# Attention, Fourier mixing and feed-forward block on one core: key memories and scores first in batch 0, half tiles in column halves, weights' sums and splits pulled ahead

## The chip, the cores and the metric

One Trainium2 chip, one core. The metric is the device time of one execution in microseconds (us); three runs of the kernel before were timed. An instruction of the trace belongs to TensorE (PE; its weight loads are PEld), VectorE (DVE), ScalarE (ACT), GpSimd (POOL) or to SyncE's DMA queue (SP).

## The reference

```python
a = exp(phi - max(phi, axis=2)); a = a / (sum(a, axis=2) + 1e-9)   # phi: B 8, H 8, S 576, M 32
k_m = einsum('bhsm,bhsd->bhmd', a, k)                              # memories, 32 per head
v_m = einsum('bhsm,bhsd->bhmd', a, v)
attn = softmax(q @ k_m.T / 8) @ v_m                                # B, H, S, D 64
x = attn.transpose(0, 2, 1, 3).reshape(B, S, 512)
u = x + real(fft(fft(x, axis=1), axis=2))
un = (u - mean(u)) / sqrt(var(u) + 1e-6)                           # over the 512
out = u + relu(un @ w_ch1) @ w_ch2                                 # 512 -> 2048 -> 512
```

## The kernel before, in words

Per batch (8 of them, 4 pairs of heads each) `background` makes attention and mixing: `pooling_weights` (the exponentials of phi, transposed), `pair_memory` (tiles pm: keys' and values' memories), `pair_scores` (tiles psc, softmax, and the even and odd sums `aeo` that the transform over tokens needs, L485 to L522), `values` (values times the transform over the model, pv, then vh), `spectrum` (pa, then at), and for each token tile `mix_m` (the mixing product pp, cosine part in columns 0 to 256 and sine part in the other 255) and `mix_x` (px, the attention output itself), added by `add_mix` (L654). A batch has 576 tokens, so four full tiles of 128 and one half tile of 64 rows; two batches share a tile with their halves.

Two token tiles form a chunk (18 chunks). Each is normed (`norm_tile`, `norm_chunk`), and goes through the feed-forward part in 8 weight blocks of 256 inner columns. Products are made from high and low f16 parts, three per product (`ffn1`, `ffn2`); batches 0 and 1 and the first chunk take f32 products instead, which the trace shows as two records each (`ffn1_direct` L712: 8 products a block, `ffn2_direct` L729: 4 a block).

The weights arrive as 64-bit words and become f32 on the chip in `to_f32`: ACT's L808, DVE's L810 and L811 (sign), and for the low word either DVE's L821, or, for the keys in the list `LP` (four blocks of the second weight), DVE's L816 and an addition on POOL (L819). Each block's squares are then summed (ACT L830, a matmul with ones in `all_sum`, tile as_sq), which gives the scale (`norm_scale`, L232 to L243); `split_w1`, `scale_w2` and `prepare_w2` make the f16 parts. The first chunk runs beside this conversion, block by block.

A scheduler places the instructions of each engine by modelled times. Its order is bent by `tc.high_priority(n)`, which pulls what is issued within it ahead, and by `tc.issue_after(x)`, which holds an instruction until x has been issued. `GATE1` and `GATE2` name for each weight block such marks: "un1" and "uh0" belong to the first chunk's norm, "s0_3" is set by the last score operation of batch 0 (L522). The small constants mk come by a DMA of SP, as do phi, the pairs, the transform tables (vt, ct) and the weights.

Of the kernel before, what the change touches and what calls it, by code (L numbers as in the profile page):

```python
# [20 lines left out]
P = 128  # L21
# [21 lines left out]
KEEP = [8, 18, 0, 0, 22, 4, 3]  # L43
GATE1 = [[]] + [["un1", "uh0"]] * 7
GATE2 = [["un1", "uh0"]] * 8
NA = 2
# [7 lines left out]
L2 = [2, 4, 6]  # L54
LP = ["2_0", "2_2", "2_4", "2_6"]
W1_STAGE = ["w4", "w6", "s1", "w6", "s1", "s2", "s1", "x"]
# [76 lines left out]
def kernel(  # L133
# [200 lines left out]
    def pooling_weights(b):  # L334
# [28 lines left out]
        for g in range(2):  # L363
# [7 lines left out]
            )  # L371

    def pair_memory(b, g, r, vmf, ivs):

# [3 lines left out]
        if b < NX:  # L378
            pm = psg.tile([P, 512], F32, tag="g", name=f"pm_{n}")
            mm = groups()  # L380
            for w in range(2):
                for t in range(NST):
                    mm(
                        pm[:, w * 64 : w * 64 + 64],
                        lhsT=kv[:, t, w, :],
                        rhs=et32[:, g // 2, t, 64 * (g % 2) : 64 * (g % 2) + 64],
                        start=(t == 0),
                        stop=(t == NST - 1),
                    )
            kmf = share[:, g * 64 : g * 64 + 64] if b == 0 else tiny("kmf", 64, 2)  # L390
            nc.vector.tensor_tensor(out=kmf, in0=pm[:, 0:64], in1=mk[:, 0:64], op=ALU.mult)
            nc.vector.tensor_tensor(
                out=vmf[:, g],
                in0=pm[:, 64:128].unsqueeze(1).to_broadcast([P, 2, 64]),
                in1=mk[:, 0:64].unsqueeze(1).to_broadcast([P, 2, 64]),
                op=ALU.mult,
            )
            return q, None, kmf, 1.0 / 8.0
        am = tiny("am", 3, 1)
# [218 lines left out]
    def mix_m(b, key, cols, rows, at, vh, beta, qscale):  # L618

        pp = psg.tile([P, 512], F32, tag="g", name=f"pp_{b}_{key}")  # L620
        mm = groups()
        for cs in range(2):
            js = slice(0, NJ) if cs == 0 else slice(NJ, DM)
            i = 0
            for kb in range(2):
                for la, lv in ((0, 0), (1, 0), (0, 1)):
                    mm(
                        pp[rows, js],
                        lhsT=at[:, (kb * 2 + cs) * 2 + la, cols],
                        rhs=vh[:, lv, kb, js],  # L630
                        start=(i == 0),
                        stop=(i == 5),
                    )
                    i += 1
        qs = qsb[qi[0] % 2]
        qi[0] += 1
        nc.scalar.activation(qs[rows, 1 : NJ - 1], pp[rows, NJ:DM], AF.Copy, scale=qscale[rows])  # L637
# [163 lines left out]
    def to_f32(stages, dst, key):  # L801
# [27 lines left out]
        sq = tiny("sq", 2, 4)  # L829
        marks["sq" + key] = nc.scalar.activation(elt.rearrange("p l c -> p (l c)").bitcast(BF16)[:, :UW], dst, AF.Square, accum_out=sq[:, 0:1])  # L830
        return all_sum(sq[:, 0:1], 1, f"sq_{key}")

# [16 lines left out]
    def prepare_w1(j):  # L849

        t = w1_f32(j)
        top = to_f32(parts_w1.pop(j), t, f"1_{j}")
        s = s1[:, j : j + 1]
        norm_scale(s, is1[:, j : j + 1], top, 1, 9, f"w1_{j}")

# [3 lines left out]
    def stage_w2(j):  # L859
        top = to_f32(parts_w2.pop(j), w2_f32(j), f"2_{j}")  # L860
        norm_scale(s2[:, j : j + 1], is2[:, j : j + 1], top, 1, 14, f"w2_{j}")

# [29 lines left out]
    def background():  # L892
# [3 lines left out]
        for b in range(B):  # L896
# [6 lines left out]
            yield (nt if half_made is None else half_made), 0  # L903
            if b == 0:
                for g in range(NG):
                    mem[g] = pair_memory(b, g, first[g], vmf, ivs)
            for step in range(NG + 2):
                if step < NG and b > 0:
                    r = load_pair(b, step)
                if step >= 2 and b > 0:  # L910
# [4 lines left out]
                if step < NG and b > 0:  # L915
                    mem[step] = pair_memory(b, step, r, vmf, ivs)
                    yield (nt if half_made is None else half_made), 0
# [33 lines left out]

    nc.sync.dma_start(out=mk, in_=mk_d)
    load_phi(0)
# [20 lines left out]
    def after(names, fn, *a):  # L974
        with ExitStack() as st:
            for m in names:
                st.enter_context(tc.issue_after(marks[m].ins))
            return fn(*a)

    gate = ["un1", "uh0"]  # L980

# [13 lines left out]
    for j in range(NW):  # L995
# [105 lines left out]
```

## Time and profile before

| | us |
|---|---|
| median of 3 runs (lowest, highest) | 981.11 (980.9, 982.27) |
| the profiled execution's own time | 980.04 |
| its span in the profile | 978.2 |

| engine | busy us | share of the span |
|---|---|---|
| PE | 937.8 | 96% |
| DVE | 570.7 | 58% |
| ACT | 456.0 | 47% |
| POOL | 229.9 | 23% |

The shares are means over stages that differ. The mean granted clock of TensorE is 0.989 of full speed. A row of the timeline is one instruction or a run of equal ones, with its start in us from the span's start, what it wrote and read, and in brackets the idle time of its engine before it and what ended that.

### The profile page before, as it was taken

The page shows a single profiled execution, that of the slowest core. Times are in us where ns is not written, and L with a number is a line of the kernel's source. Part 1 is how long each engine was busy: PE and PEld are TensorE (multiplying, and loading weights), DVE is VectorE, ACT ScalarE, POOL GpSimd, SP SyncE. Part 2 cuts the span into 40 slices and gives each one's busy share as a digit, 9 for nine tenths or more (in the row PEclk, how much of TensorE's full clock was granted, in tenths as well). Part 3 has the DMA queues.
Part 4 walks back from the last instruction along what each step waited for, and adds up shares of the span by engine and source line. Part 5 has one row for each costly group of instructions (what it writes and reads, how often), then busy time and mean ns, then how long its engine had stood idle before and what let it go on. Part 6 is the DMA issues. An engine that isn't in the chain of part 4 may idle for free.

```text
span 978.2 us, 18885 instructions
## 1 busy us (share of the span) xinstructions
PE 937.8 (96%) x7753; PEld 664.3 (68%) x7753; DVE 570.7 (58%) x1301; ACT 456.0 (47%) x910; POOL 229.9 (23%) x249
## 2 busy tenths in 40 slices
PE   9388898989999999999999999999999999999998
PEld 6256577666687667676767776767677667666664
DVE  3889958757655765776623666657655765311111
ACT  2455448695555544755431645565545543401110
POOL 1213324334221422333120223123311321300000
PEclk9699999999999999999999999999999999999999
DMA  9706564064225430465111632164214310210000
GB/s 351 282 7 265 180 173 131 1 140 122 62 50 99 116 88 29 88 127 122 39 23 36 122 107 68 44 120 122 69 44 86 79 26 29 44 44 1 23 22 22
DMA packets 115959, 88.08 MB, mean 90 GB/s; under 512 B 100385, under 2 KB 100385, under 8 KB 113825
## 3 DMA queue, kind: packets, MB, share of 16 engines
q1 hardware_dynamic: 115872, 86.87, 34.0%
q8 instruction: 61, 1.00, 0.5%
q14 instruction: 26, 0.20, 0.1%
HBM read 58.15 MB, written 9.44 MB: 69 GB/s over the span
## 4 chain that ended last, share of the span: by engine, by line
PE 82%; DVE 8%; ACT 4%; DMA 2%; issue 2%; POOL 1%; SPq 0%; DVEq 0%; POOLq 0%; ACTq 0%
PE po L765 34%; PE ph L273 33%; PE pm L273 4%; PE pp_t L273 3%; PE psc L273 2%; PE px_t L273 1%; PE pa L585 1%; DVE w1t L821 1%; DVE w2s L811 1%; PE po L729 1%; POOL scratch L678 1%; DMA rawt<-in_raw 1%; PE pf L343 1%; DVE w1t L811 1%; DVE uring L654 0%
## 5 line engine op out<-in xcount | busy, mean ns | idle before, releaser
L273 PE MATMUL ph<-unring,w1t 128*128 128x256 f16 x3264 | 389.0, 273 | 2.7 <-DMA unring<-ud 2.7
L765 PE MATMUL po<-w2s,hring 128*128 128x512 f16 x1632 | 378.6, 379 | 0.0
L273 PEld LDWEIGHTS <-w1t 128*128 128x128 f16 x3264 | 314.6, 98 | 65.8 <-DMA unring<-ud 3.2
L765 PEld LDWEIGHTS <-hring 128*128 128x128 f16 x1632 | 156.6, 98 | 158.0 <-issue 0.4
L756 DVE SCALAR_TENSOR_TENSOR hring<-ph,hring 128x512 f16<-128x512 f32 x136 | 93.0, 685 | 154.7 <-ACT hring L755 154.3
L755 ACT ACTIVATE hring<-ph 128x512 f16<-128x512 f32 x136 | 80.2, 590 | 168.3 <-PE ph L273 167.9
L501 POOL TENSOR_TENSOR aring<-aring,scratch 128x384 f32<-128x384 f32 x28 | 24.4, 870 | 202.2 <-DVE scratch L499 201.3
L678 POOL TENSOR_TENSOR scratch<-scratch,small 128x1 f32<-128x1 f32 x36 | 25.0, 700 | 155.6 <-DVE scratch L677 132.1
L273 PEld LDWEIGHTS <-stg 128*128 128x128 f16 x1152 | 44.9, 98 | 10.3 <-POOL stg L418 1.3
L495 ACT ACTIVATE aring<-aring,scratch 128x384 f32<-128x384 f32 x24 | 14.7, 612 | 70.4 <-DVE aring L494 70.4
L699 POOL TENSOR_TENSOR ud<-un,ud 128x1024 f16<-128x1024 f32 x17 | 37.5, 2203 | 29.9 <-ACT ud L698 29.9
L273 PE MATMUL pp_t<-vh,at 128*128 128x255 f16 (+3 forms) x288 | 36.6, 273 | 2.4 <-ACT at L600 1.5
L273 PE MATMUL pm<-et,stg 128*128 128x64 f16 (+1 forms) x780 | 37.0, 199 | 1.3 <-POOL stg L418 1.2
L418 POOL TENSOR_TENSOR stg<-rawt,stg 128x640 f16<-128x640 f32 x12 | 17.8, 1487 | 81.9 <-ACT rawt L417 81.9
L485 DVE TENSOR_REDUCE scratch<-psc 128x12 f32<-128x384 f32 x32 | 17.7, 552 | 32.6 <-PE psc L273 17.5
L640 DVE SCALAR_TENSOR_TENSOR share<-pp_t,scratch,small 128x257 f32<-128x257 f32 (+1 forms) x48 | 21.1, 480 | 25.3 <-ACT small L637 25.3
L729 PE MATMUL po<-w2s,hring 128*128 128x512 f32 x64 | 30.3, 600 | 4.8 <-ACT hring L715 2.9
L520 ACT CAST aeo<-eo 128x384 f16<-128x384 f32 x30 | 15.3, 511 | 41.4 <-DVE eo L517 41.2
L513 DVE TENSOR_TENSOR eo<-aring 128x128 f32<-128x128 f32 x29 | 30.8, 1063 | 5.6 <-POOL aring L511 5.6
L654 DVE SCALAR_TENSOR_TENSOR uring<-px_t,scratch,share 128x256 f32<-128x256 f32 (+1 forms) x80 | 33.9, 475 | 0.2
L777 DVE SCALAR_TENSOR_TENSOR uring<-po,small,uring 128x512 f32<-128x512 f32 x34 | 24.0, 741 | 16.5 <-PE po L765 16.5
L511 POOL TENSOR_TENSOR aring<-aring 128x128 f32<-128x128 f32 x56 | 32.7, 603 | 2.1
(240 smaller groups left out, 1232.6 us busy)
## 6 DMA issues: line engine op xcount, KB each, us to landing
rawt<-in_raw SPq DMA_DIRECT2D x15, 640.0 KB, 5.1
stg<-in_raw SPq DMA_DIRECT2D x15, 640.0 KB, 4.1
out<-uring SPq DMA_DIRECT2D x36, 256.0 KB, 2.3
stg<-in_w SPq DMA_DIRECT2D x7, 1024.0 KB, 5.7
rawt<-in_raw SPq DMA_DIRECT2D x15, 384.0 KB, 3.1
stg<-in_raw SPq DMA_DIRECT2D x15, 384.0 KB, 3.1
phs<-in_raw SPq DMA_DIRECT2D x32, 160.0 KB, 5.2
w2s<-in_w SPq DMA_DIRECT2D x4, 1024.0 KB, 9.8
```

What stands on the lines that cost most here:

```text
L273: m = nc.tensor.matmul(out, lhsT=lhsT, rhs=rhs, start=start, stop=stop)
L501: eng.tensor_tensor(out=a, in0=a, in1=sm.unsqueeze(2).to_broadcast([P, 12, M]), op=ALU.mult)
L511: eng.tensor_tensor(out=a2[:, i : i + 4], in0=a[:, 0:4], in1=a[:, 4:8], op=op)
L513: nc.vector.tensor_tensor(out=eo[:, 1:3, 0], in0=ap[:, 1:3, 0], in1=ap[:, 1:3, 1], op=ALU.add)
L654: nc.vector.scalar_tensor_tensor(out=u[rows, hs], in0=px[rows, hs], scalar=igx[rows], in1=tm[rows, w * NJ + half : w * NJ + half + 256], o ...
L678: nc.gpsimd.tensor_tensor(out=rs, in0=rs, in1=half, op=ALU.pow)
L699: marks[f"ul{c}"] = nc.gpsimd.tensor_tensor(out=ud[:, 1], in0=un, in1=ud[:, 0], op=ALU.subtract)
L729: nc.tensor.matmul(po[t], lhsT=h[:, f, t], rhs=w[:, f], start=(j == 0 and f == 0), stop=(j == NW - 1 and f == UB - 1),)
L755: nc.scalar.activation(h[:, 0], phv, AF.Relu)
L756: nc.vector.scalar_tensor_tensor(out=h[:, 1], in0=phv, scalar=0.0, in1=h[:, 0], op0=ALU.max, op1=ALU.subtract)
L765: nc.tensor.matmul(po[t], lhsT=hs[j][:, lh, f * 2 + t], rhs=w2s[:, j * UB + f, lw, :], start=(j == 0 and f == 0 and i == 0), stop=(j == NW ...
L777: nc.vector.scalar_tensor_tensor(out=u, in0=po[t], scalar=cout if c else 0.5, in1=u, op0=ALU.mult, op1=ALU.add)
```

## The change

Six edits:

- GATE1 and GATE2 of block 0 name "s0_3": the conversions of both blocks 0 stand after batch 0's last score operation, instead of anywhere (first weight) and after the first norm (second).
- `LP` is empty: no low word goes over POOL any more; the four blocks take L821's form on DVE.
- In batch 0 `memory_f32` makes the keys' half of a pair's memories, and the scores follow pair by pair; the values' halves come after all four.
- The half tile's cosine product goes into the token rows and its sine product into the other 64 rows of the same PSUM tile, by turns.
- `soon(j)` puts the squares, sums, scales and splits of blocks 1 to 7 and the two weight-2 steps at high priority.
- The DMA of mk has high priority.

```diff
-GATE1 = [[]] + [["un1", "uh0"]] * 7
-GATE2 = [["un1", "uh0"]] * 8
+GATE1 = [["s0_3"]] + [["un1", "uh0"]] * 7
+GATE2 = [["s0_3"]] + [["un1", "uh0"]] * 7
...
-LP = ["2_0", "2_2", "2_4", "2_6"]
+LP = []
...
+    def memory_f32(b, g, r, vmf, parts):
...
+        for w in parts:
...
+        if 0 in parts:
             kmf = share[:, g * 64 : g * 64 + 64] if b == 0 else tiny("kmf", 64, 2)
             nc.vector.tensor_tensor(out=kmf, in0=pm[:, 0:64], in1=mk[:, 0:64], op=ALU.mult)
+        if 1 in parts:
             nc.vector.tensor_tensor(
                 out=vmf[:, g],
...
+        half_tile = rows.stop - rows.start < P
+        sin_rows = slice(64 - rows.start, 128 - rows.start) if half_tile else rows
...
+            (nc.tensor.matmul if half_tile else mm)(
+                pp[sin_rows if cs else rows, js],
+                lhsT=at[:, (kb * 2 + cs) * 2 + la, cols],
+                rhs=vh[:, lv, kb, js],
...
+        if half_tile:
+
+            for i in range(6):
+                for cs in range(2):
+                    product(i, cs)
...
+        with soon(int(key[2:])):
+            marks["sq" + key] = nc.scalar.activation(dump, dst, AF.Square, accum_out=sq[:, 0:1])
+            return all_sum(sq[:, 0:1], 1, f"sq_{key}")
...
+        with soon(j):
+            norm_scale(s, is1[:, j : j + 1], top, 1, 9, f"w1_{j}")
...
+                for g in range(NG + 1):
+                    if g < NG:
+                        km = memory_f32(b, g, first[g], vmf, [0])
+                        mem[g] = first[g][:, KV:], None, km, 1.0 / 8.0
+                    if g > 0:
+                        ahl[g - 1] = pair_scores(b, g - 1, *mem.pop(g - 1), aeo)
                 for g in range(NG):
-                    mem[g] = pair_memory(b, g, first[g], vmf, ivs)
...
+                    memory_f32(b, g, first[g], vmf, [1])
...
-    nc.sync.dma_start(out=mk, in_=mk_d)
+    with tc.high_priority(1000):
+        nc.sync.dma_start(out=mk, in_=mk_d)
...
+    def soon(j):
+        return tc.high_priority(1000) if j else nullcontext()
...
-        split_w1(j)
+        with soon(j):
+            split_w1(j)
...
-    scale_w2()
+    with soon(1):
+        scale_w2()
...
-    prepare_w2()
+    with soon(1):
+        prepare_w2()
```

What moves on DVE in batch 0's scores (L391 and L392 are the keys' and values' memories, L485 and L494, now L494 and L503, the first two score operations of a pair, L810 to L821 the conversion of the first weight's block 0). Before:

```order
L391 TENSOR_TENSOR share<-pm_3_254,small 128x64
L392 TENSOR_TENSOR vmf<-pm_3_254,small 128x128
L810 TENSOR_SCALAR w1t<-w1t 128x1024
L485 TENSOR_REDUCE scratch<-psc_0_267 128x12
L811 SCALAR_TENSOR_TENSOR w1t<-w1t 128x1024
L494 TENSOR_TENSOR aring<-psc_0_267,scratch 128x384
```

Now:

```order
L391 TENSOR_TENSOR share<-pm_0_4_215,small 128x64
L391 TENSOR_TENSOR share<-pm_1_5_222,small 128x64
L494 TENSOR_REDUCE scratch<-psc_0_229 128x12
L503 TENSOR_TENSOR aring<-psc_0_229,scratch 128x384
L391 TENSOR_TENSOR share<-pm_2_6_253,small 128x64
```

The first score reduction stood behind all eight memory operations and a conversion; it now stands behind the keys' halves of two pairs, and no conversion is among the scores.

What stands on DVE between batch 0's last score operation and the first at (L522, now L531: aeo; L597, now L606: at). Before:

```order
L522 SCALAR_TENSOR_TENSOR aeo<-aeo,small,un 128x4x32
L522 SCALAR_TENSOR_TENSOR aeo<-aeo,small,eo 128x4x32
L597 SCALAR_TENSOR_TENSOR at<-pa_0_0_413,at 128x2x145
L597 SCALAR_TENSOR_TENSOR at<-pa_0_1_423,at 128x2x145
L597 SCALAR_TENSOR_TENSOR at<-pa_1_0_433,at 128x2x145
```

Now:

```order
L531 SCALAR_TENSOR_TENSOR aeo<-aeo,small,eo 128x4x32
L829 TENSOR_SCALAR w1t<-w1t 128x1024
L829 TENSOR_SCALAR w2s<-w2s 128x1024
L830 SCALAR_TENSOR_TENSOR w1t<-w1t 128x1024
L830 SCALAR_TENSOR_TENSOR w2s<-w2s 128x1024
L840 SCALAR_TENSOR_TENSOR w1t<-w1t 128x1024
L840 SCALAR_TENSOR_TENSOR w2s<-w2s 128x1024
L576 SCALAR_TENSOR_TENSOR vh<-pv_0_387,vh 128x512
L576 SCALAR_TENSOR_TENSOR vh<-pv_1_388,vh 128x512
L606 SCALAR_TENSOR_TENSOR at<-pa_0_0_417,at 128x2x145
```

The six conversions of blocks 0 and both vh operations now stand between aeo and at.

What moves on PE in a half tile, here batch 0's (pp_t is the half tile's product). Before, six of one width and then six of the other:

```order
L273 MATMUL pp_t_644<-vh,at 64x257
L273 LDWEIGHTS at
L273 MATMUL pp_t_644<-vh,at 64x257
L273 LDWEIGHTS at
L273 MATMUL pp_t_644<-vh,at 64x255
```

Now by turns:

```order
L637 LDWEIGHTS at
L637 MATMUL pp_t_647<-vh,at 64x257
L637 LDWEIGHTS at
L637 MATMUL pp_t_647<-vh,at 64x255
L637 LDWEIGHTS at
L637 MATMUL pp_t_647<-vh,at 64x257
```

The count of products and of weight loads stays at twelve. On PE, tile 1 of batch 0 (pp_t and 11 of its 16 px) also moves ahead of the first chunk's first ph, where it stood behind the first block's po.

## Rows read from the trace of the kernel before

**Rows 1.** Busy time by stage: us from A to B, length, engines' busy time (xcount), granted clock, DMA share, GB/s.

```profile
40.00:50.00 10.00, 4.18 (x42) 3.83 (x43) 6.66 (x17) 2.61 (x8) 2.38 (x4) 0.56 0.33 131
60.00:126.00 66.00, 56.53 (x243) 38.20 (x244) 64.65 (x98) 34.82 (x60) 19.45 (x7) 1.00 0.48 168
126.00:164.00 38.00, 38.00 (x328) 32.21 (x327) 24.81 (x80) 25.67 (x48) 15.53 (x20) 1.00 0.64 183
164.00:205.00 41.00, 33.41 (x271) 24.71 (x264) 29.78 (x79) 30.20 (x56) 13.13 (x11) 0.96 0.16 34
205.00:940.00 735.00, 733.68 (x6396) 518.84 (x6395) 408.72 (x934) 342.67 (x700) 169.71 (x190) 1.00 0.31 71
```

**Rows 2.** Timeline of DVE, 17 to 54 us: start, us, instruction, [idle before <-releaser].

```profile
18.29 0.23 DVE L391 TENSOR_TENSOR share<-pm,small 128x64 f32<-128x64 f32 x1 [4.44 <-PE pm L273]
...
24.13 0.56 DVE L485 TENSOR_REDUCE scratch<-psc 128x12 f32<-128x384 f32 x1 [0.32 <-PE psc L273]
...
41.31 1.27 DVE L567 SCALAR_TENSOR_TENSOR vh<-pv,vh 128x512 f16<-128x512 f32 x2
...
45.01 0.75 DVE L522 SCALAR_TENSOR_TENSOR aeo<-aeo,small,eo 128x128 f16<-128x128 f16 x1
49.00 1.72 DVE L597 SCALAR_TENSOR_TENSOR at<-pa,at 128x290 f16<-128x290 f32 x4 [3.23 <-ACT at L596]
53.15 0.88 DVE L640 SCALAR_TENSOR_TENSOR share<-pp_t,scratch,small 128x257 f32<-128x257 f32 x2 [2.43 <-ACT small L637]
```

**Rows 3.** Timeline of PE, 13 to 66 us.

```profile
13.71 2.34 PE L273 MATMUL pm<-et,rawt 128*128 128x64 f32 x20
...
22.59 1.50 PE L273 MATMUL psc<-share,rawt 128*128 128x64 f32 x12
...
60.41 3.72 PE L712 MATMUL ph<-unring,w1t 128*128 128x256 f32 x16 [0.67 <-ACT unring L695]
```

**Rows 4.** The tile of the small constants, first 20 us: its DMA on SP and its landing.

```profile
L952 SPq DMA_DIRECT2D small<-in_mk x1: 328/328/328, 9.2 to 9.2; - x1
...
DMA to landing us min/median/max: 9.0/9.0/9.0
```

**Rows 5.** Timeline of DVE, 55 to 130 us: operations of the weights' conversion.

```profile
58.87 0.69 DVE L816 TENSOR_SCALAR w2s<-w2s 128x1024 uint32<-128x1024 uint32 x1
...
63.89 2.90 DVE L810 TENSOR_SCALAR w2s<-w2s 128x1024 int32<-128x1024 int32 x1
...
70.19 1.21 DVE L821 SCALAR_TENSOR_TENSOR w1t<-w1t 128x1024 uint32<-128x1024 uint32 x1
...
116.05 2.40 DVE L810 TENSOR_SCALAR w1t<-w1t 128x512 int32<-128x512 int32 x1
```

**Rows 6.** Timeline of POOL, the first of the four low-word additions.

```profile
63.51 2.73 POOL L819 TENSOR_TENSOR w2s<-w2s 128x1024 int32<-128x1024 int32 x1 [5.13 <-issue]
```

**Rows 7.** Timeline of PE, 92 to 134 us: products of the first chunk.

```profile
92.92 1.88 PE L729 MATMUL po<-w2s,hring 128*128 128x512 f32 x4
94.64 1.89 PE L712 MATMUL ph<-unring,w1t 128*128 128x256 f32 x8
...
131.62 1.88 PE L729 MATMUL po<-w2s,hring 128*128 128x512 f32 x4
```

**Rows 8.** Timeline of PE, 262 to 293 us: pv, and a half tile of a later batch.

```profile
262.71 0.84 PE L558 MATMUL pv<-stg,share 64*32 64x512 f16 x24
263.49 2.03 PE L273 MATMUL ph<-unring,w1t 128*128 128x256 f16 x17
...
291.01 1.50 PE L273 MATMUL pp_t<-vh,at 128*64 128x257 f16 x12
292.35 0.61 PE L273 MATMUL px_t<-vbdt,attnT 128*64 128x128 f16 x8
```

**Rows 9.** Costliest groups by shape: weight loads of the half tiles (busy us, mean ns | idle before).

```profile
L273 PEld LDWEIGHTS <-at 128*64 128x64 f16 x96 | 9.9, 110 | 4.4 <-issue 2.5 <-ACT at L600 1.8
```

**Rows 10.** Timeline of ACT, 133 to 136 us: squares of a weight block.

```profile
133.55 1.06 ACT L830 ACTIVATE elt<-w1t 128x1024 bf16<-128x1024 f32 x1 [1.28 <-PE as_sq L223]
```

More of the change, by code (lines that the diff above doesn't have):

```diff
@@ L371, in pooling_weights @@
             )
-    def pair_memory(b, g, r, vmf, ivs):
-        n = f"{b}_{g}"
+    def memory_f32(b, g, r, vmf, parts):
         kv = r[:, :KV].rearrange("p (t w c) -> p t w c", t=NST, w=2)
-        q = r[:, KV:]
[L378 to L389, printed above, removed]
+        pm = psg.tile([P, 512], F32, tag="g", name=f"pm_{b}_{g}_{len(kept)}")
+        kept.append(pm)
+        mm = groups()
+        for w in parts:
+            for t in range(NST):
+                mm(
+                    pm[:, w * 64 : w * 64 + 64],
+                    lhsT=kv[:, t, w, :],
+                    rhs=et32[:, g // 2, t, 64 * (g % 2) : 64 * (g % 2) + 64],
+                    start=(t == 0),
+                    stop=(t == NST - 1),
+                )
+        kmf = None
+        if 0 in parts:
             kmf = share[:, g * 64 : g * 64 + 64] if b == 0 else tiny("kmf", 64, 2)
             nc.vector.tensor_tensor(out=kmf, in0=pm[:, 0:64], in1=mk[:, 0:64], op=ALU.mult)
+        if 1 in parts:
             nc.vector.tensor_tensor(
@@ L397, in pair_memory @@
             )
-            return q, None, kmf, 1.0 / 8.0
+        return kmf
+    def pair_memory(b, g, r, vmf, ivs):
+        n = f"{b}_{g}"
+        kv = r[:, :KV].rearrange("p (t w c) -> p t w c", t=NST, w=2)
+        q = r[:, KV:]
+        if b < NX:
+            return q, None, memory_f32(b, g, r, vmf, range(2)), 1.0 / 8.0
         am = tiny("am", 3, 1)
@@ L621, in mix_m, with product @@
         mm = groups()
-        for cs in range(2):
+        half_tile = rows.stop - rows.start < P
+        sin_rows = slice(64 - rows.start, 128 - rows.start) if half_tile else rows
+        def product(i, cs):
+            kb, (la, lv) = i // 3, ((0, 0), (1, 0), (0, 1))[i % 3]
             js = slice(0, NJ) if cs == 0 else slice(NJ, DM)
[L624 to L634, printed above, removed]
+            (nc.tensor.matmul if half_tile else mm)(
+                pp[sin_rows if cs else rows, js],
+                lhsT=at[:, (kb * 2 + cs) * 2 + la, cols],
+                rhs=vh[:, lv, kb, js],
+                start=(i == 0),
+                stop=(i == 5),
+            )
+        if half_tile:
+            for i in range(6):
+                for cs in range(2):
+                    product(i, cs)
+        else:
+            for cs in range(2):
+                for i in range(6):
+                    product(i, cs)
         qs = qsb[qi[0] % 2]
         qi[0] += 1
-        nc.scalar.activation(qs[rows, 1 : NJ - 1], pp[rows, NJ:DM], AF.Copy, scale=qscale[rows])
+        nc.scalar.activation(qs[rows, 1 : NJ - 1], pp[sin_rows, NJ:DM], AF.Copy, scale=qscale[sin_rows])
         tm = share
@@ L829, in to_f32 @@
         sq = tiny("sq", 2, 4)
-        marks["sq" + key] = nc.scalar.activation(elt.rearrange("p l c -> p (l c)").bitcast(BF16)[:, :UW], dst, AF.Square, accum_out=sq[:, 0:1])
-        return all_sum(sq[:, 0:1], 1, f"sq_{key}")
+        dump = elt.rearrange("p l c -> p (l c)").bitcast(BF16)[:, :UW]
+        with soon(int(key[2:])):
+            marks["sq" + key] = nc.scalar.activation(dump, dst, AF.Square, accum_out=sq[:, 0:1])
+            return all_sum(sq[:, 0:1], 1, f"sq_{key}")
     def w1_f32(j):
@@ L853, in prepare_w1 @@
         s = s1[:, j : j + 1]
-        norm_scale(s, is1[:, j : j + 1], top, 1, 9, f"w1_{j}")
+        with soon(j):
+            norm_scale(s, is1[:, j : j + 1], top, 1, 9, f"w1_{j}")
     def w2_f32(j):
@@ L860, in stage_w2 @@
         top = to_f32(parts_w2.pop(j), w2_f32(j), f"2_{j}")
-        norm_scale(s2[:, j : j + 1], is2[:, j : j + 1], top, 1, 14, f"w2_{j}")
+        with soon(j):
+            norm_scale(s2[:, j : j + 1], is2[:, j : j + 1], top, 1, 14, f"w2_{j}")
     def scale_w2():
@@ L904, in background @@
             if b == 0:
+                for g in range(NG + 1):
[4 more added lines that the diff above has]
+                        ahl[g - 1] = pair_scores(b, g - 1, *mem.pop(g - 1), aeo)
                 for g in range(NG):
-                    mem[g] = pair_memory(b, g, first[g], vmf, ivs)
-            for step in range(NG + 2):
-                if step < NG and b > 0:
+                    memory_f32(b, g, first[g], vmf, [1])
+            for step in range(NG + 2) if b > 0 else ():
+                if step < NG:
                     r = load_pair(b, step)
-                if step >= 2 and b > 0:
+                if step >= 2:
                     pair_transpose(b, step - 2, ahl.pop(step - 2), attnT)
@@ L914, in background @@
                     yield (nt if half_made is None else half_made), 0
-                if step < NG and b > 0:
+                if step < NG:
                     mem[step] = pair_memory(b, step, r, vmf, ivs)
@@ L1001 @@
         ffn2_direct(j, po)
-        split_w1(j)
+        with soon(j):
+            split_w1(j)
         advance(0, steps=STEPS)
```

## Prediction

> **What bounds the kernel now.** I read the busy time by stage first. From 205 to 940 us PE is busy 733.68 of 735.00 us [rows 1]: there only fewer or shorter PE instructions save time, and a faster DVE, ACT or POOL saves nothing. In 126 to 164 us PE has no gap either. In 60 to 126 us it is another picture: PE idles 66.00 - 56.53 = 9.5 us while DVE is busy 64.65 of 66.00 [rows 1]; this is where the first chunk runs beside the weights' conversion, and DVE paces it. In 40 to 50 us PE is busy 4.18 of 10 us at a granted clock of 0.56 [rows 1], as it waits for the end of batch 0's scores. In 164 to 205 us it idles 7.6 us.
>
> Then the timelines. On DVE the first score reduction of batch 0 starts at 24.13, the last score operation ends at 45.01 + 0.75 = 45.76, and at, which the mixing needs, follows at 49.00 and ends at 50.72 [rows 2]. The chain from there runs through the first two token tiles and their norm to the first ph on PE at 60.41 [rows 3]. The last po of the first chunk starts at 131.62 and takes about 1.7, so PE leaves the chunk at 133.34 (the profile adds pipeline time to a record's length: four po take 94.64 - 92.92 = 1.72 from start to start [rows 7]).
>
> **The sum, part by part.** It is made against the profiled execution, 980.04 us, which is 1.07 under the median of 981.11.
>
> *Key memories and scores first, conversions behind them.* A pair's memory product shows 20 records in 2.18 from start to start (half is the keys': 1.09), and its scores take 1.34 (22.59 to 23.93 by the start of the next pair's) [rows 3]. The keys' products of two pairs and the first scores then end at 13.71 + 1.09 + 1.09 + 1.34 = 17.2, and the first reduction can start at about 17.3 instead of 24.13. It needs mk: its DMA was issued at 9.2 and landed 9.0 later, at 18.2, and the first memory operation started at 18.29 although its product had long been there [rows 2, 4]. With high priority it is issued eighth on SP's queue, two or three places behind the first pair's loads; from 0.33 an issue I estimate 5.5, so a landing at 14.5. Bounds: if it landed at 18.2 again, the products made first would all wait, and the start would be some 3.4 later; issued any earlier nothing more is gained, since then the products set the start. SP's loads behind it (a pair's query half, the next pair, the tables) go 0.33 later each and are wanted some us later than they land.
>
> The chain of scores from the first reduction to the last score operation takes 45.76 - 24.13 = 21.6 on DVE. It loses two conversions of 1.2 and the vh operations (1.2) [rows 2, 5] and gains the keys' halves of two pairs (0.45) and the four values' operations (0.8, four at 0.2 by the starts), and I add 1.0 for scores that DVE now waits for: 20.4. So aeo is ready at 17.3 + 20.4 = 37.7 instead of 45.8. But behind it now stand six conversions, two at 0.6 and four at 1.14 from start to start (0.69 and 1.21 as records [rows 5]), 5.8 in all, and vh, 1.2, and only then at: 37.7 + 5.8 + 1.2 + 1.7 = 46.4, some 4 ahead of 50.72. ACT now has the conversion's first steps and two squares at 1.06 [rows 10] among its copies; I take 0.5 off for them. The gain for the first mixing is 3.5. The price of the conversions here is not lost: they stood between the norm and the first products. The first ph moves by 3.5, and back by 1.4 for the mixing of tile 1 that now stands ahead of it on PE (about 2.1 of work, of which 0.67 fills the wait in front of ph [rows 3]): 60.41 - 3.5 + 1.4 = 58.3.
>
> *No low words on POOL, block 0 of the second weight early.* While POOL runs an addition of 1024 (63.51 to 66.24 [rows 6]), DVE's shift beside it takes 2.90 instead of 0.69 [rows 5]. There are four such stretched operations, the first and last of which stand in the rows, 10.6 us in all; at 0.69 they would take 2.8, so 7.8 go. The low word costs DVE 1.21 in place of 0.69, four times: 2.1 more. Three operations of block 0 (about 3) have moved out of the stretch. DVE's 64.65 become some 56.
>
> So PE can pace this stretch. Its work from the first ph to the last po: a block shows 16 records of ph and 8 of po, four times 1.72 [rows 7], so 8 blocks take 55.0. Before, PE was busy 56.53 + 7.34 = 63.9 from 60 to 133.34 [rows 1, 7], which leaves 8.9 of other work; without tile 1's mixing (2.4) and half of the half tile (0.7), 5.9. With 1.3 for the first waits, PE could leave the chunk at 58.3 + 55.0 + 5.9 + 1.3 = 120.5, 12.8 earlier. I take **10**: a block's conversion, three operations of 0.69 + 1.21 + 1.21 = 3.1, still starts only when its load has landed in an area that an earlier conversion frees, and I let PE wait for one of them. Bounds: 12.8 with no wait, 6 if the waits (9.5 before) stay at half their size and the start at its bound for mk.
>
> *Squares, sums, scales, splits at high priority.* They bring nothing of their own in the sum: before 133 us they are behind the first po's in need, and after it PE has no gap until 164. If they come early, the gaps of 164 to 205 (7.6) could shrink; if they crowd ACT, the batch 1 chain behind them gets longer. Bounds 3 lost, 5 won; I take 0, since in the order the last sums and the weight-2 splits keep their places relative to batch 1's work.
>
> *Half tiles.* Twelve products take 292.35 - 291.01 = 1.34, 0.112 each [rows 8]. By turns they go to the two column halves of the array. That parts of the array run together shows in pv: 24 products of 512 columns, each on an eighth of the array, take 0.78, while 17 of 256 on the whole array take 2.03 [rows 8], at which rate 24 of 512 would take 5.7. Two at a time give 6 x 0.112 = 0.67, so 0.67 less per half tile. Of eight half tiles six lie where PE has no gap (batch 0's is counted above, batch 1's lies among gaps): 6 x 0.67 = **4.0**. Nothing else is late there: the sine part's copy reads other partitions of the same tile. Bounds 0 (they queue) and 4.7 (batch 1's counts as well).
>
> The weight loads between them don't show in this: the twelve products follow each other at 0.112 with twelve weight loads between them, which take 110 ns each [rows 8, 9] and so are hidden behind products of the same rows of the array. The Trainium skill (TensorE: Matmul & The Clock Gate, Part 3: Packing small matmuls) says that a weight load overlaps with running products only when their row groups differ, and here both column halves use all rows. The trace's own half tiles don't agree with it.
>
> Sum: 980.04 - 10 - 4.0 = 966.0; with 1.07 for the median, **967**. By its own bounds (6 to 12.8, 0 to 4.7, 3 lost to 5 won, not all at once) 961 to 971.
>
> **The rivals.**
> 1. *The column halves don't run together.* For it: in pv the eight tiles also differ in rows, so no row shows two column halves alone. Against it: four of pv's eight share their rows, and still more than seven ran at a time. Time: 967 + 4 = 971.
> 2. *Loads in sequence.* If each product waited for its own load, a half tile took 12 x (0.11 + 0.11) = 2.65 instead of 1.34, 1.3 more in six places instead of 0.67 less: 967 + 4 + 7.8 = 979. The 0.112 from start to start with the loads between them speaks against it [rows 8, 9]. The Trainium skill's rule named above would have it so.
> 3. *The gain is given back.* PE reaches the second chunk 10 us earlier, but batch 1's scores, norm and ACT's splits do not, and the gaps of 164 to 205 grow. For it: PE idles 7.6 there already, behind chains on DVE and ACT [rows 1]. Against it: 126 to 164 is dense, and DVE there is busy only 24.81 of 38. With 7 of the 10 given back: 974.
> 4. *Slower: sums that hold PE.* The as_sq products stand in PE's queue early, each behind a square on ACT of 1.06 [rows 10] that itself waits for DVE's conversion. PE takes its instructions in order, so every block's products behind such a sum would wait for a conversion that they did not need yet. There are 16 sums; against a gain of 14 it decides from a mean wait of 14 / 16 = 0.9 on, and at 1.2 to 1.4 the time is 986 to 990. For it: before, PE waited on such chains already (9.5 us of gaps). Against it: in the order the sums stand behind the first products of their own block, mostly after the conversion that both need.
>
> A case of its own is that batch 0's start, DVE's relief and the later gaps all pay fully: 958 to 961.
>
> **How the numbers follow.** Forecast 0.58, rival 1 0.12, rival 2 0.05, rival 3 0.15, rival 4 0.06, the larger gain 0.04. The range is 959 to 977: it takes in the forecast's bounds, rivals 1 and 3, and leaves out rivals 2 and 4 and the tail of the larger gain. A measurement of this kernel can tell about 0.2% (2 us) from no change. Faster by more than that: all but rivals 2 (half of it) and 4 and a little of 3, 0.90; within 0.2%: 0.04; slower: 0.06.
>
> **What would show it.** In the profile of the changed kernel: the first score reduction at about 17.3 and the last aeo at about 37.7; the first ph near 58, the last f32 po ending near 123; no POOL addition during the conversions and no conversion on DVE over 1.3 us; PE idle in the first chunk of some 4 us instead of 9.5; a half tile's twelve products in about 0.7 us; the stretch after the first chunk unchanged in its gaps. It is wrong if as_sq is what ends PE's waits, if the half tiles still take 1.3, if mk still lands at 18, or if the gaps between the first chunk and 205 us grow by what the chunk has gained.

## The result and the profile after

| | before | changed |
|---|---|---|
| median, us | 981.37 | 967.02 (965.78 to 967.57) |
| ratio, 95% interval | | 0.9851 (0.9834 to 0.9868) |
| the profiled execution's own time, us | 980.04 | 966.73 |
| its span, us | 978.2 | 964.8 |
| PE busy, us | 937.8 | 936.0 |
| PE idle (span less busy), us | 40.4 | 28.8 |

The forecast was 967. Two terms of its sum came out a little larger than forecast, and one that it had put at 0 took that back. Of the 13.4 us of span, 11.6 are idle time of PE. Its busy time fell by only 1.8 although the half tiles alone save more, since it was busy for longer at the lower clock (below).

Busy time by stage of the changed kernel (from and to, length, PE, PEld, DVE, ACT, POOL busy, granted clock, DMA share, GB/s):

```profile
57.00:115.00 58.00, 54.20 (x218) 36.41 (x217) 54.51 (x89) 31.00 (x56) 5.90 (x3) 0.97 0.57 199
...
126.00:164.00 38.00, 31.93 (x302) 27.93 (x300) 28.98 (x87) 27.16 (x53) 19.89 (x24) 0.96 0.52 133
164.00:205.00 41.00, 38.30 (x318) 27.75 (x319) 28.19 (x73) 31.46 (x60) 13.50 (x10) 0.96 0.26 57
205.00:926.00 721.00, 720.74 (x6308) 508.49 (x6307) 407.37 (x922) 334.15 (x683) 163.48 (x186) 1.00 0.30 70
```

Against [rows 1]: the tail is PE's alone, as before; the first chunk (57 to 115) has 3.8 us of PE idle; and 126 to 164, which had no gap, now has 6.1, while 164 to 205 has 2.7 instead of 7.6. The gaps between the first chunk and 205 us have moved forward and add up to 8.8 instead of 7.6.

DVE in batch 0 (start, us, instruction), against [rows 2]:

```profile
17.12 0.56 DVE L494 TENSOR_REDUCE scratch<-psc 128x12 f32<-128x384 f32 x1 [1.12 <-PE psc L273]
...
36.08 0.75 DVE L531 SCALAR_TENSOR_TENSOR aeo<-aeo,small,eo 128x128 f16<-128x128 f16 x1
36.75 0.68 DVE L829 TENSOR_SCALAR w1t<-w1t 128x1024 int32<-128x1024 int32 x1
...
42.50 1.28 DVE L576 SCALAR_TENSOR_TENSOR vh<-pv,vh 128x512 f16<-128x512 f32 x2
43.70 1.58 DVE L606 SCALAR_TENSOR_TENSOR at<-pa,at 128x290 f16<-128x290 f32 x4
...
91.92 2.88 DVE L840 SCALAR_TENSOR_TENSOR w1t<-stg,w1t 128x1024 uint32<-128x1024 uint32 x1
```

The scores start 7.0 us sooner and end 8.9 sooner; the six conversions then take 5.75, and at ends 5.4 us ahead of before. The last row is a conversion of the first weight that took 2.88 instead of 1.21. No low word runs on POOL any more, but something on POOL still stretches DVE there (below).

PE of the changed kernel, first and last direct products, their one long wait, and a later half tile, against [rows 3, 7, 8]:

```profile
44.23 2.52 PE L273 MATMUL pp_t<-vh,at 128*128 128x257 f16 x12
...
56.52 3.67 PE L731 MATMUL ph<-unring,w1t 128*128 128x256 f32 x16
...
95.06 5.38 PE L731 MATMUL ph<-unring,w1t 128*128 128x256 f32 x16 [2.41 <-DVE w1t L840]
...
122.67 1.69 PE L273 MATMUL ph<-unring,w1t 128*128 128x256 f16 x14
124.20 1.88 PE L748 MATMUL po<-w2s,hring 128*128 128x512 f32 x4
...
282.98 0.85 PE L637 MATMUL pp_t<-vh,at 128*64 128x257 f16 x12
283.66 0.61 PE L273 MATMUL px_t<-vbdt,attnT 128*64 128x128 f16 x8
```

A half tile's products take 283.66 - 282.98 = 0.68 instead of 1.34. The last po of the first chunk now starts in the row at 124.20, so PE has done with the chunk at 124.20 + 1.72 = 125.9. In the kernel before, 133.34 is not that point, though the prediction takes it for it: half a block's po, 4 of the 64 records, stand behind products of the second chunk and of batch 1 there:

```profile
138.22 1.08 PE L729 MATMUL po<-w2s,hring 128*128 128x512 f32 x2
...
139.16 1.10 PE L729 MATMUL po<-w2s,hring 128*128 128x512 f32 x2
```

So the two ends can't be compared as they stand, but points of equal work can. PE's busy time and the count of its products from the start to two such points (the first group behind the length), before and changed:

```profile
0.00:133.36 133.36, 105.74 (x601) 73.60 (x602) 102.41 (x204) 56.12 (x107) 31.51 (x30) 0.94 0.61 214
0.00:199.79 199.79, 164.59 (x1106) 120.77 (x1106) 153.89 (x353) 105.76 (x197) 56.84 (x58) 0.95 0.52 173
```

```profile
0.00:122.66 122.66, 106.76 (x602) 74.52 (x603) 96.18 (x207) 57.83 (x108) 17.49 (x26) 0.94 0.66 233
0.00:191.17 191.17, 166.69 (x1106) 121.49 (x1107) 146.78 (x353) 106.30 (x197) 43.82 (x54) 0.95 0.54 180
```

Counted by tile, too, the products are the same at both points, but for one small sum as_sq at the first. So PE is 10.7 us ahead of the kernel before when the first chunk is nearly done, and 8.6 ahead in the second chunk: 2.1 are lost between the two. Behind the second point 4.8 us come on top, made of six half tiles (0.66 each, 4.0) and a wait of 1.2 for a pm that is gone, less 0.4 of small shifts. Together that is the 13.4. In the second profile of the changed kernel the two leads are 12.2 and 9.8.

PE's waits in the whole stretch from 56 to 205 us (for what, us in total, times, longest), of the changed kernel:

```profile
PE pp_t L637 <- ACT at L609: 3.4, 1, 3.4
PE ph L273 <- DVE scratch L232: 2.8, 1, 2.8
PE ph L731 <- DVE w1t L840: 2.4, 1, 2.4
PE ph L273 <- DMA unring<-ud: 1.7, 1, 1.7
PE po L748 <- ACT hring L734: 1.4, 1, 1.4
...
```

The wait of 2.8 for a ph of the second chunk (at 150) is new; the one of 3.4 for the half tile of batch 1 was 1.5 before. A wait of 3.3 for aeo in front of batch 1's pa, the longest before, is gone.

The stretches in which the granted clock is half and PE works, before and changed (here the clock is the third number from the end, 0.50: 1.2 of 2.4 GHz):

```profile
31.70:48.80 17.10, 5.74 (x54) 3.58 (x55) 13.96 (x38) 6.64 (x14) 6.95 (x8) 0.50 0.69 224
168.20:171.60 3.40, 3.38 (x23) 2.79 (x22) 2.63 (x5) 3.40 (x7) 0.13 (x1) 0.50 0.00 0
```

```profile
31.50:38.30 6.80, 3.17 (x36) 1.41 (x37) 6.80 (x20) 3.62 (x6) 2.69 (x4) 0.50 1.00 287
45.10:48.60 3.50, 3.50 (x25) 2.82 (x24) 0.88 (x3) 2.72 (x6) 0.00 (x0) 0.51 0.01 3
96.30:99.80 3.50, 3.50 (x10) 2.79 (x9) 3.50 (x9) 1.35 (x5) 0.00 (x0) 0.51 1.02 269
151.00:154.40 3.40, 3.40 (x18) 2.35 (x16) 2.35 (x8) 0.94 (x3) 1.03 (x2) 0.51 0.46 74
164.60:168.00 3.40, 3.40 (x28) 2.50 (x23) 1.47 (x7) 0.47 (x1) 0.41 (x1) 0.50 0.00 0
```

Half of PE's busy time in them is lost: 9.12 / 2 = 4.6 us before, 16.97 / 2 = 8.5 now, 3.9 more. So busy and idle time add up: idle time -11.6, eight half tiles at 0.66 -5.3, clock +3.9, together -13.0 of the 13.4. This is bookkeeping and not a list of causes: in batch 0's start, where the first of these stretches lie, PE also waits for other engines, and what it does more slowly there can shorten a wait instead of making the kernel longer. Nor is it steady: in the second profile of the changed kernel the half clock takes 5.7 instead of 8.5, and that execution took 965.61 us.

### The profile page after: what moved, and what is told of

Its sections match the earlier page's. It is cut to its first block, busy times and chain, and to the rows that moved or that the text cites. A ratio compares the mean times of both kernels' runs of the same rounds, so it can differ in the third digit from the quotient of the medians.

```text
span 964.8 us, 18884 instructions
## 1 busy us (share of the span) xinstructions
PE 936.0 (97%) x7753; PEld 661.1 (69%) x7753; DVE 567.5 (59%) x1301; ACT 456.3 (47%) x910; POOL 214.4 (22%) x245
## 4 chain that ended last, share of the span: by engine, by line
PE 84%; DVE 8%; ACT 3%; DMA 2%; issue 1%; POOL 1%; SPq 0%; DVEq 0%; POOLq 0%; ACTq 0%
PE ph L273 35%; PE po L784 34%; PE pm L273 3%; DMA phs<-in_raw 2%; PE pp_t L273 2%; PE psc L273 2%; PE px_t L273 2%; PE po L748 1%; PE ph L731 1%; PE keep L251 1%; PE pa L594 1%; DVE w1t L840 1%; DVE w2s L830 1%; PE pp_t L637 1%; PE pv L567 1%
## 5 line engine op out<-in xcount | busy, mean ns | idle before, releaser
L697 POOL TENSOR_TENSOR scratch<-scratch,small 128x1 f32<-128x1 f32 x36 | 21.1, 591 | 172.8 <-DVE scratch L696 139.9
L427 POOL TENSOR_TENSOR stg<-rawt,stg 128x640 f16<-128x640 f32 x12 | 17.3, 1438 | 94.1 <-ACT rawt L426 94.1
L731 PE MATMUL ph<-unring,w1t 128*128 128x256 f32 x128 | 31.9, 396 | 2.4 <-DVE w1t L840 2.4
L522 DVE TENSOR_TENSOR eo<-aring 128x128 f32<-128x128 f32 x29 | 28.9, 997 | 5.9 <-POOL aring L520 5.9
L494 DVE TENSOR_REDUCE scratch<-psc 128x12 f32<-128x384 f32 x32 | 17.7, 552 | 24.1 <-PE psc L273 12.6
L731 PEld LDWEIGHTS ph<-unring,w1t 128*128 128x128 f32 x128 | 25.0, 199 | 9.8 <-issue 6.4
```

What stands on the lines that cost most here:

```text
L522: nc.vector.tensor_tensor(out=eo[:, 1:3, 0], in0=ap[:, 1:3, 0], in1=ap[:, 1:3, 1], op=ALU.add)
L731: nc.tensor.matmul(ph, lhsT=w[:, k, f * P : (f + 1) * P], rhs=unTs[0][:, k], start=(k == 0), stop=(k == NK - 1))
```

## The experiments

Each starts from the changed kernel and was measured beside the kernel before, which had medians of 981.0 to 981.9 us in the four sets. Idle is span less PE busy in the profile.

| run | median, us | ratio to before, 95% interval | PE idle |
|---|---|---|---|
| changed kernel | 967.02 | 0.9851 (0.9834 to 0.9868) | 28.8 |
| half tiles put back | 973.09 | 0.9912 (0.9893 to 0.9930) | 30.7 |
| low words on POOL again | 974.64 | 0.9931 (0.9916 to 0.9946) | 34.0 |
| no high priority | 963.45 | 0.9816 (0.9798 to 0.9835) | 27.2 |
| gates put back | 969.30 | 0.9871 (0.9847 to 0.9895) | 29.2 |
| batch 0 put back | 972.72 | 0.9911 (0.9892 to 0.9929) | 34.0 |
| half tiles not by turns | 966.70 | 0.9853 (0.9837 to 0.9869) | 29.1 |
| no priority, second gate put back | 966.53 | 0.9851 (0.9832 to 0.9870) | 29.3 |
| no priority, dummies in a gap | 969.67 | 0.9883 (0.9858 to 0.9909) | 29.2 |
| changed kernel again | 966.25 | 0.9846 (0.9829 to 0.9863) | 29.1 |
| no high priority again | 961.45 | 0.9795 (0.9782 to 0.9809) | 25.7 |
| no priority for squares alone | 967.01 | 0.9849 (0.9833 to 0.9864) | 29.4 |
| no priority, low parts on DVE | 959.41 | 0.9774 (0.9761 to 0.9788) | 22.9 |

**Half tiles put back.**

```diff
-        half_tile = rows.stop - rows.start < P
+        half_tile = False
```

Expected: 

> The half tiles alone are put back: both products of a half tile go to the token rows again, six of one width and then six of the other. Theory (two column halves run together): twelve products last 1.23 us from the first start to the last instead of 0.57, all eight tiles, 0.66 each; where PE is bound this is 4.0 to 5.3 us, so 971 to 972.5 us. Rival (the half tiles gave nothing, the gain lies in the first 205 us): 966.5 to 968. PE's idle time stays near 36 us with the theory.

Measured 973.09, 6 to 7 us over the two measurements of the changed kernel and 0.6 above the theory's range. A half tile's twelve products are back at 1.34 us (0.66 more, eight times 5.3); the trace also has 1.6 to 1.9 us more idle time, for the scheduler orders other work differently after the longer product. The theory's mechanism holds. The 36 us of idle time that it names were wrong: the changed kernel has 28.8, this one 30.7.

**Half tiles not by turns.** Both column halves, but six cosine products and then six sine products in the queue.

```diff
-        if half_tile:
+        if False:
             for i in range(6):
                 for cs in range(2):
                     product(i, cs)
```

Expected: 

> The half tiles keep the two column halves, but the six cosine products come first and then the six sine products, no longer by turns. Theory (two products overlap only where neighbours in the queue lie in different halves): twelve products take 1.1 to 1.25 us from first to last start, as in the kernel before, and the time is 970.5 to 972.5. Rival (it is the division of the rows, or a reordering by PE, that makes it faster): 0.57 us and 966.5 to 968.

Measured 966.70: the theory fell on its time. PE at a half tile (start, us, instruction):

```profile
282.06 0.87 PE L637 MATMUL pp_t<-vh,at 128*64 128x257 f16 x10
282.74 0.22 PE L273 MATMUL px_t<-vbdt,attnT 128*64 128x128 f16 x1
282.77 0.27 PE L637 MATMUL pp_t<-vh,at 128*64 128x255 f16 x1
282.80 0.28 PE L273 MATMUL px_t<-vbdt,attnT 128*64 128x128 f16 x2
282.88 0.27 PE L637 MATMUL pp_t<-vh,at 128*64 128x255 f16 x1
282.91 0.44 PE L273 MATMUL px_t<-vbdt,attnT 128*64 128x128 f16 x5
```

The px stand behind all twelve pp_t in the queue, and three of them start before the last pp_t do: a product whose column half is free starts ahead of one whose half is busy. So the division of the rows makes the gain, and turns are hardly needed: the pp_t themselves spread over 0.82 us from first to last start instead of 0.57, but the px run beside their end.

**Low words on POOL again.**

```diff
-LP = []
+LP = ["2_0", "2_2", "2_4", "2_6"]
```

Expected: 

> LP alone is put back: four low words of the second weight go over POOL's addition again. Theory (POOL's additions stretch the DVE operations beside them, and DVE paces the first chunk, where it is busy 54.5 of 58 us now): about 6 us more DVE time, of which PE shows 4 to 7 us as waits before the first chunk's ph and po; 971 to 974 us. Rival (PE's waits there come from the loads of the weight blocks, so DVE has room): 967 to 968.

Measured 974.64, 8 us over the changed kernel, just above the theory's range. An L838 addition on POOL, a conversion beside it, and PE's wait:

```profile
93.58 3.31 POOL L838 TENSOR_TENSOR w2s<-w2s 128x1024 int32<-128x1024 int32 x1 [1.22 <-DVE w2s L830]
```

```profile
94.57 3.41 DVE L840 SCALAR_TENSOR_TENSOR w1t<-stg,w1t 128x1024 uint32<-128x1024 uint32 x1
```

```profile
98.03 6.29 PE L731 MATMUL ph<-unring,w1t 128*128 128x256 f32 x14 [4.11 <-DVE w1t L840]
```

The conversion takes 3.41 instead of the changed kernel's 2.88 (1.21 where nothing disturbs it), and PE waits 4.11 for it instead of 2.41. At the first point of equal work PE is 6.4 us ahead of the kernel before instead of 10.7 to 12.2, so some 4 to 6 of the 8 us are lost up to there and the rest behind it. In all PE idles 5.2 us more (34.0 against 28.8), and by the sum above the half clock takes 2.1 more.

**Gates put back.** GATE1 and GATE2 as they were.

```diff
-GATE1 = [["s0_3"]] + [["un1", "uh0"]] * 7
-GATE2 = [["s0_3"]] + [["un1", "uh0"]] * 7
+GATE1 = [[]] + [["un1", "uh0"]] * 7
+GATE2 = [["un1", "uh0"]] * 8
```

Expected: 

> The two gates of block 0 alone are put back, so that the first weight's block 0 may stand among batch 0's scores and the second weight's only after the first norm. Theory: three DVE operations (3 us) return into the first chunk, where DVE is the bound, and two conversions (2.3 us) into the scores, while the at operations come some 3.5 us sooner after the last score operation: 967 to 971 us, the first po later by about 3 us. Rival (the six conversions ahead of vh and at hold the first mixing by more than they save): 962 to 966.

Measured 969.30, in the theory's range and above the rival's. The first ph comes 1.1 us sooner (55.41), and the first po then waits 2.81, to 61.95. The profile puts that wait to ACT's hring, which starts at 61.54 behind five first steps of conversions (block 0 of the second weight among them) and a split; that block itself is converted at 60.73. By the medians the gates bring some 2 to 3 us, but the intervals of the ratio overlap (0.9847 to 0.9895 here, 0.9834 to 0.9868 and 0.9829 to 0.9863 for the changed kernel), so the size isn't clear of the noise.

**No priority, second gate put back.** The same question without the high priority, for the second weight alone.

```diff
-GATE2 = [["s0_3"]] + [["un1", "uh0"]] * 7
+GATE2 = [["un1", "uh0"]] * 8
...
-        return tc.high_priority(1000) if j else nullcontext()
+        return nullcontext()
```

Expected: 

> Without the high priority, and with the second weight's block 0 gated behind the first norm again; the first weight's block 0 stays behind the scores. Theory: three conversions (2.9 us) leave the stretch between the last score operation and at, so the first ph comes some 2.5 us sooner; they return to the first chunk, where DVE has some room, so 961 to 964.5 us against 963.45 with the high priority alone taken away. Rival (DVE paces the first chunk fully): 965 to 967.

Measured 966.53, 3 to 5 over the two measurements without the high priority: the rival. The first ph does come 2.5 us sooner (54.79 against 57.3), but the first po waits 2.83 for ACT's hring, and at the first point of equal work PE is 10.0 us ahead of the kernel before instead of 11.7 to 11.9. Conversions taken out of the time before the first ph return in the first chunk and cost more there.

**Batch 0 put back.** Memories of all pairs first, keys and values together.

```diff
-                for g in range(NG + 1):
-                    if g < NG:
-                        km = memory_f32(b, g, first[g], vmf, [0])
...
                 for g in range(NG):
-                    memory_f32(b, g, first[g], vmf, [1])
+                    mem[g] = pair_memory(b, g, first[g], vmf, ivs)
...
```

Expected: 

> Batch 0 alone is put back: keys' and values' memories of all four pairs first, then the scores (the gates stay, so the six conversions still stand behind the scores). Theory (the start of the scores carries through to the first ph): the first score reduction at about 24 instead of 17.1, the values' operations (0.8 us) out of the chain, so the first ph some 5 to 6 us later, at about 62; 971 to 974 us. Rival (DVE's conversions pace the first chunk whenever it starts, so the later start is made up): 967 to 969.

Measured 972.72. The first score reduction is at 24.39, the first ph at 62.65, 6.1 later than in the changed kernel, and the time is 5.7 to 6.5 us above the two measurements of the changed kernel: as the theory has it. In this kernel mk's DMA is issued behind the table ct again, at 9.3, though its high priority is still there; and the changed kernel without that priority alone has the same order on every engine, row for row (it was not run). What brought mk forward is its earlier reader, not its priority.

**No high priority**, measured in two sets.

```diff
-        return tc.high_priority(1000) if j else nullcontext()
+        return nullcontext()
```

Expected: 

> The high priority of squares, sums, scales and splits is taken away, all else stays. Theory (it brings nothing of its own): 966 to 968.5 us. Rival 1 (squares and splits that stand ahead on ACT and DVE make the new waits at 150 us, 2.84 us, and the two additional stretches of granted clock 0.5, 1.7 us each): faster without it, 960 to 964. Rival 2 (it lets the second chunk start early, and the gain of the first chunk would be given back without it): 971 to 977, with PE idle between 126 and 205 us up by 4 us or more.

Expected in the second set, for the changed kernel: 

> The changed kernel itself, on the same chip as the next three. Theory (the high priority costs time): 2 to 5 us above the run without it. Rival (the two agree, and what the first runs showed was their spread): within 1 us of it.

and without the priority: 

> The changed kernel without the high priority once more, on the same chip as the changed kernel. Theory: 962 to 964.5 us, 2 to 5 us under the changed kernel. Rival: within 1 us of the changed kernel, 965 to 967.5.

Measured 963.45, and in the second set 961.45 against 966.25 of the changed kernel, with intervals of the ratio that lie apart (0.9782 to 0.9809, 0.9829 to 0.9863). The high priority costs 4 to 5 us. The stretch from 126 to 205 us loses them. PE's waits there, changed kernel and without the priority, in the second set:

```profile
PE pp_t L637 <- ACT at L609: 3.4, 1, 3.4
PE ph L273 <- DVE scratch L232: 2.8, 1, 2.8
PE ph L273 <- DMA unring<-ud: 1.7, 1, 1.7
PE po L784 <- DVE uring L673: 0.9, 1, 0.9
```

```profile
PE pa L586 <- DVE aeo L531: 3.3, 1, 3.3
PE pp_t L637 <- ACT at L609: 1.5, 1, 1.5
PE ph L273 <- DVE vmf L453: 0.5, 1, 0.5
```

8.8 us against 5.3. The wait for at is shorter by 1.9, the one at 150 is gone: there PE runs 48 products of ph in a row (146.06 to 151.39) where it had stopped after 8. Half of PE's busy time in the half-clock stretches is 5.7 us in the one trace of this set and 5.6 in the other, so the waits alone make the difference; the clock, the other half of rival 1, isn't needed for it. Equal work says the same: without the priority PE is 11.7 and 13.5 us ahead of the kernel before at the two points, with it 12.2 and 9.8. Up to the end of the first chunk the priority does nothing, and behind it a gain of 1.8 becomes a loss of 2.4.

**No priority for the squares alone**, scales and splits keep it.

```diff
-        with soon(int(key[2:])):
+        with nullcontext():
             marks["sq" + key] = nc.scalar.activation(dump, dst, AF.Square, accum_out=sq[:, 0:1])
```

Expected: 

> The high priority is taken from the squares and their sums alone; scales, splits and the two steps on the second weight keep it. Theory (the squares ahead on ACT are what makes the wait of 2.84 us at 150): 962 to 964.5 us, and no such wait. Rival (the splits ahead on ACT and DVE do it): 966 to 968, with the wait.

Measured 967.01: neither theory. The wait at 150 is gone as the first had it, but others stand in its place (2.6 for a pm, 1.9 for a pl), and the time is the changed kernel's. The reverse, the priority on the squares alone, gives the changed kernel's order on DVE and ACT but for a few rows; it was not run. So the priority costs the same with or without that of the squares; which of the pulled instructions does it isn't told.

**No priority, dummies in a gap.** `soon` as in the run without the priority, and beside it:

```diff
+            if b == 1:
+                pk = psg.tile([P, 512], F32, tag="g", name="keep_b1")
+                for _ in range(24):
+                    nc.tensor.matmul(pk[:, :NKP], lhsT=ident, rhs=ct[:, 0, 0], start=True, stop=True)
             at = spectrum(b, aeo)
```

Expected: 

> Without the high priority, and with 24 products of 290 columns that nobody reads, put on PE between pv and pa of batch 1, where PE idles 3.08 us. Theory (a gap of some 3 us is followed by 3.4 us at granted clock 0.5, which costs 1.7 us of PE's work): the clock stays at 1 around 152 to 160 us, 961 to 963 us against 963.45 without them. Rival (the dummies only fill a gap): 963 to 964.

Measured 969.67, slower, and inconclusive on the price of the clock. The dummies ran in the gap (152.39 to 155.36) and the clock stayed up in what followed, but the scheduler, which counts them as work, put other instructions elsewhere, and PE waits 3.5 us for a transposed input and 2.3 for a split of POOL instead.

**No priority, low parts on DVE.** Since one conversion was still stretched, its neighbour on POOL, the low parts of the second chunk's normed input, goes to DVE. `soon` is again as in the run without the priority.

```diff
-    marks[f"ul{c}"] = nc.gpsimd.tensor_tensor(out=ud[:, 1], in0=un, in1=ud[:, 0], op=ALU.subtract)
+    marks[f"ul{c}"] = (nc.vector if c == 1 else nc.gpsimd).tensor_tensor(out=ud[:, 1], in0=un, in1=ud[:, 0], op=ALU.subtract)
```

Expected: 

> Without the high priority, and with the low parts of the second chunk's normed input made by DVE instead of POOL (that subtraction runs on POOL for 4.80 us beside the conversion, and stretches one DVE operation to 2.88 us instead of 1.21). Theory (as with the low words: it is cheaper on DVE while DVE paces the chunk): DVE gains 1.7 and pays some 1.2, PE's wait of 2.4 us for the conversion falls below 2, and the second chunk's input is ready sooner; 961 to 963 us. Rival (DVE pays as much as it gains): 963 to 965.

Measured 959.41 (959.17 to 961.04), ratio 0.9774: the fastest of all and below the theory's range, 2 us under the same kernel with the subtraction on POOL in this set and 4 under it in the other. In this set the executions don't overlap (959.17 to 961.04, 961.12 to 963.21), though the intervals of the ratio just touch. Little else of DVE's order differs. With it on POOL (POOL, DVE, PE):

```profile
89.72 4.80 POOL L718 TENSOR_TENSOR ud<-un,ud 128x1024 f16<-128x1024 f32 x1 [5.64 <-ACT ud L717]
```

```profile
92.72 2.89 DVE L840 SCALAR_TENSOR_TENSOR w1t<-stg,w1t 128x1024 uint32<-128x1024 uint32 x1
```

```profile
95.86 3.69 PE L731 MATMUL ph<-unring,w1t 128*128 128x256 f32 x16 [2.40 <-DVE w1t L840]
```

and on DVE (DVE, PE):

```profile
91.88 1.21 DVE L840 SCALAR_TENSOR_TENSOR w1t<-stg,w1t 128x1024 uint32<-128x1024 uint32 x1
...
93.61 1.21 DVE L718 TENSOR_TENSOR ud<-un,ud 128x1024 f16<-128x1024 f32 x1
```

```profile
93.34 3.69 PE L731 MATMUL ph<-unring,w1t 128*128 128x256 f32 x16 [0.71 <-DVE w1t L840]
```

The same subtraction takes 1.21 on DVE and cost 1.68 of DVE's time when POOL made it. Here it also moves behind the conversion that PE needs next.

## Why the prediction was right, point by point

- **The start of batch 0** was right: first reduction 17.12 (17.3 forecast), last aeo at 36.83 (37.7), at done at 45.3 (46.4), first ph 56.52 (58.3). mk was issued at 6.3 and landed 8.1 later, at 14.4 (14.5), but the prediction ascribed that to its high priority, which does nothing here. That the scores carry through to the end is shown by putting batch 0 back: some 6 us.
- **The relief of DVE**, with that start, was right in its mechanism and in its size: 10.7 us at equal work (12.2 in the second profile) where 10 was taken. The first chunk has the idle time that was forecast, 3.8 us ("some 4"): one wait for a conversion (2.4, taken at 2.8) and one for an hring (1.4, where 1.3 stood for first waits). The reading of 133.34 as the chunk's end was wrong, as shown above: by then only 60 of the 64 po records had been made, so the "8.9 of other work" were 10.6. The slip cancels, since the 120.5 worked out from it is then the same point of the changed kernel, which measured 122.67. A stretch at half clock (96.3 to 99.8, 1.75 us) was missing from the sum, and is inside the 10.7. The statement "no conversion on DVE over 1.3 us" failed: POOL's subtraction of the second chunk stretched one to 2.88. The trace of before had the same thing, a conversion of 3.15 at 100.17 beside that subtraction, and the prediction counted only the four additions. With the additions back the time is 8 us longer.
- **The half tiles** were right: 0.68 against 0.67 forecast. The sum had them six times, and the six bring 0.66 each (1.23 to 0.57 from the first start to the last). Batch 0's goes from 1.20 to 0.57, batch 1's only from 1.23 to 0.74, as part of it runs at half clock. Rival 1 (the halves don't run together) is refuted, and so is rival 2, the loads in sequence: the half tile has twelve loads of all rows in its 0.68 us. The Trainium skill (TensorE: Matmul & The Clock Gate, Part 3: Packing small matmuls), where it lists what overlaps, has loads overlap with running products only for differing row groups; this case's trace does not agree.
- **Squares, sums, scales and splits** were mis-sized: the sum took 0, with bounds of 3 lost and 5 won, and they lose 4 to 5, a little beyond the lower bound. The reason stood there as "if they crowd ACT, the batch 1 chain behind them gets longer", and in rival 3, which puts the loss between the first chunk and 205 us. That is where it lies. Rival 3 as a whole did not come true: of the lead at the end of the first chunk 2.1 to 2.4 us are given back, not 7. That the gaps there stay unchanged, as the prediction had it, failed (8.8 for 7.6, at other places and for other waits). Rival 4's mechanism, PE held by as_sq, doesn't show: no as_sq stands among PE's waits.
- **The clock** had no term. PE lost 3.9 us more to it than before in the one profile and 1.1 more in the other; how much of that is in the time isn't shown, beyond the stretch in the first chunk.

In the sum: 10.7 for 10, -2.1 for 0, 4.8 for 4.0, so 13.4 for 14.0. That the time met the forecast to 0.02 us is luck, since the errors have both signs; that it came within some 2 us is not luck, as each term but one was met to 1 us.

## What to carry to other kernels

Where one engine paces a stage, look at who runs beside it before you count its work: an operation sent from DVE to POOL to spare DVE half a microsecond took some two from it, and taking back the additions brought 8 us, the last subtraction 2 to 4. High priority for work that was on no critical path took places here from work that was: of the six edits it was the one that cost, and it was seen only by taking it out alone. A product that fills half of the array's columns has a free partner in the other half, in whatever order the two stand.

## What the runs showed of the hardware

- Products in different column halves of the array pass each other: with the six sine products queued behind six cosine products, the first px started before the last two sine products that stood ahead of it.
- An operation on DVE that a POOL operation stretches looks like one that waits for it to end, and not like one that runs slower. In the three rows shown, POOL ends at 66.24 [rows 6], 96.89 and 94.52, and the DVE operation beside it at 66.79 [rows 5], 97.98 and 95.61: 0.55, 1.09 and 1.09 later, about what the same operations take from start to start when undisturbed (0.6 and 1.14). DVE operations that ran wholly within POOL's time kept their usual length (1.21 for the L830 at 90.72 in the last of the three). So the price is how far the one operation reaches back into POOL's, some 2 us here, and it falls on whatever stands next on DVE. No run tests this by itself.
- Gaps of PE and the clock are loosely bound: the changed kernel had the same wait of 2.4 us before the ph at 95 in both of its profiles, once with a clock of 0.66 over the 5 us from 95 on, once with 1.00:

```profile
95.00:100.00 5.00, 4.94 (x15) 4.10 (x16) 5.00 (x11) 1.35 (x5) 0.00 (x0) 0.66 1.03 259
```

```profile
95.00:100.00 5.00, 4.70 (x19) 3.72 (x20) 5.00 (x11) 1.73 (x6) 0.00 (x0) 1.00 1.00 223
```

  The 16 records of ph took 5.38 us in the first and 3.69 in the second. The stretch takes 1.75 us of PE's work (3.50 / 2 above), and the executions of this kernel spread over 3.7 us (965.45 to 969.16); how much of the spread comes from such stretches isn't shown.
